# The last expert stage's first product for two batches at a time, as a 2x2x2 block product with seven products

## The chip, the core and the metric

The kernel runs on one core of one Trainium2 chip. The metric is device time in microseconds (us), the median of several runs of one kernel. Engines are called by the profile's names: PE (TensorE), DVE (VectorE), ACT (ScalarE), POOL (GpSimd) and SP (SyncE, which issues every DMA here).

## The reference

```python
x = attention(q, k, v)                   # 4 batches x 448 rows, 12 heads x 64 = 768 columns
h = x @ w_in;  g = h * cos(h)            # first expert stage, 768 -> 2048
y = g @ w_out                            # 2048 -> 768
a = y @ w1;  b = y @ w2                  # last expert stage, 768 -> 1024 each
out = ((a * b) @ w3) @ w_out2            # 1024 -> 1024 -> 768
```

All in float32. The host hands the weights over as 64-bit floats, which the kernel turns into float32 on the chip.

## The kernel before, in words

Data lie transposed: a tile has 128 columns of the activations as its partitions and the 448 rows of a batch along it. Every exact product is made of three matmuls on two-part numbers (`mm3`, lines 356 to 359): high weight by high data, high weight by low data, low weight by high data, 128 by 128 by 448 each. A high part is a copy to the `float32r` type (`copy`, line 331), a low part the difference (`lo`, line 349).

The program has three stretches: attention; the first expert stage (`moe1`, line 903), which works in units of two column blocks and one batch, first for batches 0 and 1, then for 2 and 3; and the last expert stage (`moe2`, line 1032). The product w3 by w_out2, called w34, is made during attention (`make_w34`) and kept in DRAM, so the last stage has two products: y by [w1|w2], then (a * b) by w34.

In the last stage `ab_unit` (line 1053) makes, for a batch b and a block fc of 128 columns, both a and b: six k-steps of three matmuls each, 18 matmuls to a PSUM bank and 36 to the unit. One bank is copied to `a32`, the other multiplied by it, and the result split into `ab` high and low. `o_unit` (line 1069) then adds ab by w34 into six PSUM banks, three matmuls to each, 18 to the unit; the banks are emptied to `ob` after the eighth block and written out. The order is batch 2, 3, 0, 1; unit fc of `ab` stands before `o_unit` of the unit ahead of it. The sums y of batches 2 and 3 are split where they arise (`split_y`, line 893, called in `y_part`); those of 0 and 1 come back from DRAM (`yA_d`) when their turn is near. The weights w1 and w2 are converted (`f64`, line 796: ACT or POOL, POOL or DVE, two DVE instructions, then the split) and stay in SBUF for all four batches, blocks 0 to 3 in the pool `lp`, early, the others in `q2`, whose space is free only when the first expert stage has ended. The same holds for w34.

PSUM has eight banks. Everything is issued in an order that a planner works out before (`Plan.schedule`, line 169): each operation has a due time, a list of engines that could do it with a cost on each, and the buffers it reads and writes; the planner walks through time and gives each engine the due operation that is ready. On the chip each engine goes through its own list strictly in that order, and semaphores hold an instruction until what it reads is there.

Of the kernel before, what the change touches and what calls it, by code (L numbers as in the profile page):

```python
# [10 lines left out]
F32 = mybir.dt.float32  # L11
F32R = mybir.dt.float32r
# [22 lines left out]
TWOPI = 6.283185  # L35

# [33 lines left out]
class Ring:  # L70
    def __init__(self, plan, pool, tag, shape, dtype, n):
        self.pool, self.tag, self.shape, self.dtype = pool, tag, list(shape), dtype
        self.tiles, self.queue = {}, []
        self.free = [(0.0, k) for k in range(n)]
        plan.rings.append(self)
        pool.rings.append(self)

    def tile(self, k):
        if k not in self.tiles:
            self.tiles[k] = self.pool.pool.tile(self.shape, self.dtype, name=f"{self.tag}{k}", bufs=1)  # L80
        return self.tiles[k]
# [226 lines left out]
def program(  # L308
# [47 lines left out]
    def mm3(out, wh, wl, xh, xl, first, last):  # L356
        PE.matmul(out, wh, xh, start=first, stop=False)  # L357
        PE.matmul(out, wh, xl, start=False, stop=False)  # L358
        PE.matmul(out, wl, xh, start=False, stop=last)  # L359
# [12 lines left out]
    for name, kw in dict(const={}, xring={}, dram=dict(space=DRAM), psum=dict(space=PSUM), attn={}, lp={},  # L372
                         wi=dict(side="right"), wp=dict(side="right"), yp=right, mp=right, cv=right,
                         qp=right, q2=right).items():
        pool(name, **kw)

    def ring(p, tag, shape, dtype=F32, n=2):
        return Ring(plan, pools[p], tag, shape, dtype, n)
# [48 lines left out]
    yA_d = Scratch("dram", [BH, KD, P, S], "yA_d")  # L427
# [27 lines left out]
    xh_r = ring("xring", "xh", [P, KD, S], F32R)  # L455
    xl_r = ring("xring", "xl", [P, KD, S], F32R)
# [339 lines left out]
    def f64(due, raw_r, x_r, src, n, hi, lw, spill=None):  # L796

        r = raw_r.ref()[:, :2 * n]
        x = x_r.ref()[:, :n]
# [24 lines left out]
        plan.op(due - 5, [("DVE", 0.07 + n / 960, low, True)], r=[r, x], w=[x])  # L824
        if spill is not None:
            dma(due - 4, spill, x, r=[x], w=[spill], kb=393, write=True)
# [12 lines left out]
    def hl(p, tag, shape, n):  # L839
        return [ring(p, tag + t, shape, F32R, n) for t in "hl"]  # L840
# [49 lines left out]

    yh, yl = {}, {}

    def split_y(b, m, due, src):
        if m == 0:
            yh[b], yl[b] = xh_r.new(), xl_r.new()
        th, tl = (z[b].at(m, lambda t: t[:, m, :]) for z in (yh, yl))
        copy(due, th, src, S, "ADP")
        lo(due, tl, src, th, S)
# [4 lines left out]
    def moe1(raw_r, x_r):  # L903
# [62 lines left out]
        def y_part(u, m, due):  # L966
# [18 lines left out]
            if u == of[b][-1] and b < BH:  # L985
                z = yA_d.at((b, m), lambda d: d[b, m])
                dma(due + 3, z, ya, r=[ya], w=[z], kb=230, write=True)
            if u == of[b][-1] and b >= BH:
                split_y(b, m, due + 2, ya)
# [40 lines left out]
    EARLY12, EARLY34 = 4, 2  # L1030

    def moe2():
        raw_r, x_r = ring("lp", "rawl", [P, 2 * DM], U32, 2), ring("lp", "xl_", [P, DM], F32, 2)
        a_r, ob_r = ring("qp", "a32", [P, S], F32, 2), ring("qp", "ob", [P, S], F32, 3)
        ab_r = hl("qp", "ab", [P, S], 2)
        V0, pu = unit_due(4 * NP) + G["pu"], G["pu"]
        order = [BH + r for r in range(BH)] + list(range(BH))
        w12t, w34t, ab, acc = {}, {}, {}, {}
        for k in range(2):
            for fc in range(NF2):  # L1040
                early = fc < EARLY12
                if early == (k == 0):
                    for a in range(2):
                        w12t[fc, a] = [ring("lp" if early else "q2", f"w12{t}{fc}{a}", [P, DM], F32R, 1).ref() for t in "hl"]
                        due = V0 - 90 + 20 * fc + 10 * a if early else V0 + (fc - 1) * pu / 2
                        f64(due, raw_r, x_r, w12[fc, a], DM, *w12t[fc, a])
                early = fc < EARLY34
# [115 lines left out]
```

## Time and profile before

| | us |
|---|---|
| median of three runs | 1142.82 (1141.08 to 1144.59) |
| span of the profiled execution, first to last instruction | 1139.2 |
| what lies around the span: the median less the span | 3.6 |
| PE busy in it | 1112.9 (98%) |
| DVE, ACT, POOL busy | 740.5, 454.2, 133.3 |

The page gives no time of its own for the profiled execution beside its span. A matmul row's duration holds its way through the array and overlaps the next one, so what a matmul costs is read from start to start. The span falls into attention with the making of w34 (to about 490 us), the first expert stage (to 781 us) and the last one (781 to 1131 us, then the last writes).

### The profile page before, as it was taken

The numbers are of one execution on the slowest core, as the hardware profiler recorded it, in microseconds if no ns is written. First come the engines' busy times: TensorE is split into PE (matmuls) and PEld (weight loads), VectorE is DVE, ScalarE is ACT, GpSimd is POOL, SyncE is SP. The second block draws the span as 40 slices with busy tenths as digits, with TensorE's granted clock in tenths as the row PEclk, the third lists the DMA queues.
The fourth block names the chain that finished last, engine by engine and source line by source line (L and its number), as shares of the span: only waits on it lengthen the run. The fifth ranks groups of instructions, "written<-read, shape, count | busy, mean of one in ns | idle before, by whom it ended". The sixth has DMA issues, their size and how long they took to land.

```text
span 1139.2 us, 13718 instructions
## 1 busy us (share of the span) xinstructions
PE 1112.9 (98%) x5184; PEld 966.5 (85%) x5184; DVE 740.5 (65%) x1111; ACT 454.2 (40%) x581; POOL 133.3 (12%) x130
## 2 busy tenths in 40 slices
PE   5999999999999999999999999999999999999997
PEld 3777777778888888889999999998999999999996
DVE  5888777899998897787899877768831311311111
ACT  4887767877566655722454211113211101101001
POOL 2312111123231110110121000001200000000000
PEclk9999999999999999999999999999999999999999
DMA  8885765878756554337745211101401101101001
GB/s 231 229 224 149 212 185 171 231 210 252 209 154 188 190 148 158 130 100 235 272 127 180 70 56 56 29 1 69 140 15 41 57 1 41 57 1 40 10 1 51
DMA packets 83165, 140.10 MB, mean 123 GB/s; under 512 B 35986, under 2 KB 63634, under 8 KB 83090
## 3 DMA queue, kind: packets, MB, share of 16 engines
q1 hardware_dynamic: 83090, 139.14, 40.7%
q8 instruction: 42, 0.69, 0.2%
q14 instruction: 33, 0.27, 0.1%
HBM read 109.45 MB, written 29.58 MB: 122 GB/s over the span
## 4 chain that ended last, share of the span: by engine, by line
PE 93%; DVE 2%; DMA 1%; ACT 1%; SPq 1%; issue 0%; POOL 0%; ACTq 0%; DVEq 0%
PE bank L357 13%; PE bank L358 13%; PE bank L359 13%; PE double L358 12%; PE double L359 12%; PE double L357 12%; PE bank L595 12%; PE double L574 3%; PE double L575 3%; DMA rawc<-in_w_out 1%; SPq L353 1%; DMA kr<-in_k 0%; DVE w L343 0%; ACT double L584 0%; ACT p L584 0%
## 5 line engine op out<-in xcount | busy, mean ns | idle before, releaser
L343 DVE TENSOR_TENSOR a<-double,a 128x448 f32<-128x448 f32 x32 | 20.0, 625 | 240.1 <-PE double L359 237.7
L595 PE MATMUL bank<-p,v 112*128 112x448 f32 x384 | 161.3, 543 | 0.5 <-issue 0.5
L359 PE MATMUL double<-xh,w12l 128*128 128x448 f32 x378 | 137.8, 365 | 0.0
L358 PE MATMUL double<-xl,w12h 128*128 128x448 f32 x378 | 137.8, 365 | 0.0
L357 PE MATMUL double<-xh,w12h 128*128 128x448 f32 x378 | 137.4, 363 | 0.0
L584 ACT ACTIVATE double<-double,ts 112x896 f32<-112x896 f32 x96 | 94.1, 981 | 79.1 <-PE double L575 78.9
L333 ACT COPY a<-double 128x448 f32<-128x448 f32 x31 | 16.5, 533 | 254.1 <-PE double L359 254.1
L357 PE MATMUL bank<-xh,wih 128*128 128x448 f32 x270 | 107.9, 399 | 0.0
L595 PEld LDWEIGHTS bank<-p,v 112*128 112x128 f32 x384 | 72.6, 190 | 41.2 <-issue 38.3
L357 PE MATMUL bank<-gh,woh 128*128 128x448 f32 x260 | 102.1, 393 | 0.3 <-ACT hs L333 0.3
L358 PE MATMUL bank<-xl,wih 128*128 128x448 f32 x270 | 98.3, 364 | 0.0
L359 PE MATMUL bank<-xh,wil 128*128 128x448 f32 x270 | 98.0, 363 | 0.0
L584 ACT ACTIVATE p<-double,pac 112x896 f32<-112x896 f32 x96 | 96.7, 1010 | 2.0
L358 PE MATMUL bank<-gl,woh 128*128 128x448 f32 x260 | 95.2, 366 | 0.0
L359 PE MATMUL bank<-gh,wol 128*128 128x448 f32 x260 | 94.8, 365 | 0.0
L574 PE MATMUL double<-qh,ks 128*112 128x448 f32 x192 | 73.7, 384 | 14.4 <-DVE ks L343 10.3
L343 DVE TENSOR_TENSOR y<-bank,y 128x448 f32<-128x448 f32 x111 | 68.6, 619 | 23.0 <-PE bank L359 22.2
L358 PEld LDWEIGHTS double<-xl,w12h 128*128 128x128 f32 x378 | 71.0, 188 | 5.8
L357 PEld LDWEIGHTS double<-xh,w12h 128*128 128x128 f32 x378 | 70.8, 187 | 5.6
L359 PEld LDWEIGHTS double<-xh,w12l 128*128 128x128 f32 x378 | 71.0, 188 | 5.0
L575 PE MATMUL double<-ql,ks 128*112 128x448 f32 x192 | 72.1, 375 | 0.0
L357 PEld LDWEIGHTS bank<-xh,wih 128*128 128x128 f32 x270 | 50.8, 188 | 9.0 <-issue 5.0
(153 smaller groups left out, 2359.2 us busy)
## 6 DMA issues: line engine op xcount, KB each, us to landing
rawc<-in_w_out SPq DMA_DIRECT2D x16, 768.0 KB, 5.6
rawl<-in_w SPq DMA_DIRECT2D x16, 768.0 KB, 4.4
qr<-in_q SPq DMA_DIRECT2D x48, 224.0 KB, 4.6
kr<-in_k SPq DMA_DIRECT2D x48, 224.0 KB, 4.9
rawc<-in_w_in SPq DMA_DIRECT2D x13, 768.0 KB, 5.0
raw<-in_w3T SPq DMA_DIRECT2D x16, 512.0 KB, 5.8
raw<-in_w_out SPq DMA_DIRECT2D x8, 768.0 KB, 7.2
wo_d<-wx SPq DMA_DIRECT2D x16, 384.0 KB, 4.4
```

Source lines behind the costliest of these rows:

```text
L333: "A": ("ACT", (0.051 if psum else 0.094) + n / 1200, lambda: ACT.copy(dst(), src())),
L343: "D": ("DVE", 0.068 + n / 960, lambda: DVE.tensor_tensor(dst(), a(), b(), op=op))
L353: plan.op(due, [("SP", 0.66, lambda: SP.dma_start(dst(), src()))], r=r, w=w, kb=kb)
L357: PE.matmul(out, wh, xh, start=first, stop=False)
L358: PE.matmul(out, wh, xl, start=False, stop=False)
L359: PE.matmul(out, wl, xh, start=False, stop=last)
L574: PE.matmul(o, w, qh(), start=True, stop=False)
L575: PE.matmul(o, w, ql(), start=False, stop=True)
L584: lambda f=f, x=x, o=o: ACT.activation(o(), s(), f, scale=x[:CP]))],
L595: PE.matmul(pv()[:, :S], w()[:, 2 * c + n].rearrange("p a d -> p (a d)"), p()[:, n, :], start=c == 0 and n == 0, stop=c == NT - 1 and n == 1)
```

## The change

y of two batches is taken as a matrix of 2 by 2 blocks: rows are the two batches, columns the halves of the 768 (three k-steps each). [w1|w2] of a block fc is the other: rows are the halves, columns w1 and w2. Their product, four banks of 18 matmuls times two batches before, is made from seven products of nine matmuls (`PRODUCTS`, in Winograd's form). The left operands `A11, A12, A22` are blocks of y, `S1` to `S4` sums of them, made once for each pair of batches (`lefts`); the right operands `B11, B21, B22` and `T1` to `T4` are made for each block fc, and again for the second pair (`rights`). Operands on both sides are split into high and low parts. The products are added up partly in PSUM, where a bank is read in between and then added to further (`ab_step`), and partly by DVE.

All four batches' y now go through DRAM (`y_d`). The converted w1 and w2 are written to DRAM for the first pair (`w12_d`) and read back for the second; w34 is read again for each of its 32 uses. Right operands lie in the ring `xring` (two slots), left ones in `lp` and `q2`. In the steps of a pair, `o_unit` of the pair's first batch goes between the products; its last block and all eight of the second batch follow after the pair's last step. Some tiles begin 64 bytes further on than their slot (`PAD // 2` of four bytes): the right operands, `A22` and `ab`. In the layout of the program before, start addresses modulo 128 bytes were 32 for y and for w1, w2 of blocks 0 to 3, and 96 for those of blocks 4 to 7, for `ab`, and for w34 of blocks 2 to 7 (32 for blocks 0 and 1). In the program now every moving operand of the last stage starts at 32 and every stationary one at 96.

```diff
-    def __init__(self, plan, pool, tag, shape, dtype, n):
...
+    def __init__(self, plan, pool, tag, shape, dtype, n, shift=0):
...
+        if not self.shift:
+            return self.flat(k)
+        t, n = self.flat(k), math.prod(self.shape[1:])
+        t = t[:, self.shift % PAD:self.shift % PAD + n]
...
+            shape = [self.shape[0], math.prod(self.shape[1:]) + PAD] if self.shift else self.shape
...
-    xh_r = ring("xring", "xh", [P, KD, S], F32R)
+    xh_r = ring("xring", "xh", [P, KD, S], F32R, 2, 0 if general else PAD)
...
-            if u == of[b][-1] and b < BH:
-                z = yA_d.at((b, m), lambda d: d[b, m])
+            if u == of[b][-1]:
+                z = y_d.at((b, m), lambda d: d[b, m])
                 dma(due + 3, z, ya, r=[ya], w=[z], kb=230, write=True)
-            if u == of[b][-1] and b >= BH:
...
+    KH, HALF = KD // 2, DM // 2
+    LEFT = ("A11", "A12", "S2", "S1", "S3", "S4", "A22")
+    RIGHT = ("B11", "B21", "T1", "T3", "T2", "T4", "B22")
+    PRODUCTS = (("A11", "B11"), ("A12", "B21"), ("S2", "T2"), ("S1", "T1"), ("S3", "T3"), ("S4", "B22"), ("A22", "T4"))
     def moe2():
...
+        raws = [ring("lp", "rawl", [P, 2 * DM], U32, 1), ring("q2", "rawq", [P, 2 * DM], U32, 1)]
+        sts = [ring("lp", "stl", [P, DM], F32, 4), ring("q2", "stq", [P, DM], F32, 2)]
+        left_r = {x: hl("q2" if x == "A22" else "lp", f"y{x}", [P, KH, S], 1, PAD // 2 * (x == "A22")) for x in LEFT}
+        w34_r, ab_r = hl("q2", "w34", [P, DM], 3), hl("q2", "ab", [P, S], 3, PAD // 2)
+        c_r, tmp_r, ob_r = (ring("q2", t, [P, S], F32, n) for t, n in (("c", 11), ("tmp", 6), ("ob", 5)))
+        V0, AB, OU = unit_due(4 * NP) + G["pu"], 63 * MM, 18 * MM
+        left, right, cs = {}, {}, {}
+        def lefts(p, due, step, raw_r, st_r, late=False):
...
+            for k in range(KH):
+                t = due + k * step
...
+                raw = raw_r.new()
+                a11, a21, a12 = (raw.at(n, lambda t, n=n: t[:, n * S:(n + 1) * S].bitcast(F32)) for n in range(3))
+                a22, s3 = st_r.ref()[:, :S], st_r.ref()[:, :S]
+                for x, n, m in ((a11, 0, k), (a21, 1, k), (a12, 0, k + KH), (a22, 1, k + KH)):
+                    load(x, n, m)
+                to("A11", a11, t)
+                to("A12", a12, t + 1)
+                tt(t + 2, s3, a11, a21, S, ALU.subtract, "PD")
+                tt(t + 2, a21, a21, a22, S, ALU.add, "PD")
+                tt(t + 3, a11, a21, a11, S, ALU.subtract, "PD")
+                tt(t + 4, a12, a12, a11, S, ALU.subtract, "PD")
+                to("S2", a11, t + 4)
+                to("S1", a21, t + 3)
+                to("S3", s3, t + 4)
+                to("S4", a12, t + 5)
...
+        def seg(z, i, n):
...
+            return z.ring.flat(z.slot)[:, PAD // 2 + i * HALF:PAD // 2 + (i + n) * HALF]
...
+        def rights(p, fc, due):
+            x = [sts[0].ref(), sts[0].ref()]
             for a in range(2):
+                z = w12_d.at((fc, a), lambda d, a=a: d[fc, a])
+                if p == 0:
+                    convert(due + 2 * a, raws[a if fc else 0], x[a], w12[fc, a], DM)
+                    dma(due - 4, z, x[a], r=[x[a]], w=[z], kb=393, write=True)
+                else:
+                    dma(due - 12, x[a], z, r=[z], w=[x[a]], kb=393)
+            t13, t24 = (sts[1 if fc or p else 0].ref() for _ in range(2))
...
+            (b11, b21), (b12, b22) = ((part(r, 0), part(r, 1)) for r in x)
+            (t1, t3), (t2, t4) = ((part(r, 0), part(r, 1)) for r in (t13, t24))
+            tt(due - 3, t1, b12, b11, HALF, ALU.subtract, "PD")
+            tt(due - 2, t3, b22, b12, HALF, ALU.subtract, "PD")
+            tt(due - 2, t2, b22, t1, HALF, ALU.subtract, "PD")
+            tt(due - 1, t4, b21, t2, HALF, ALU.subtract, "PD")
+            w = right[p, fc] = xh_r.new(), xl_r.new()
...
+            to(0, 2, x[0], due - 3)
+            to(6, 1, b22, due - 2)
+            to(4, 2, t24, due)
+            to(2, 2, t13, due - 1)
+        def product(p, fc, i, bank, first, due):
+            a, b = PRODUCTS[i]
+            j = RIGHT.index(b)
+            x, w = left[p, a], right[p, fc]
+            def f():
+                xt = [z.tile() for z in x]
+                wt = [seg(z, j, 1) for z in w]
+                for k in range(KH):
+                    c = slice(k * P, (k + 1) * P)
+                    mm3(bank()[:, :S], wt[0][:, c], wt[1][:, c], xt[0][:, k, :], xt[1][:, k, :],
+                        first and k == 0, k == KH - 1, on=not first)
+            plan.op(due, [("PE", 9 * MM, f)], r=[*(z.at(k) for z in x for k in range(KH)), *(z.at(2 * (j // 2)) for z in w)],
+                    w=[bank])
+        def ab_step(p, fc, due, between):
+            at = [due + i * (AB + OU) / 7 for i in range(8)]
...
+            p1 = hy_r.ref()
+            product(p, fc, 0, p1, True, at[0])
+            s1 = out(p1, at[1])
+            p2 = hy_r.ref()
+            product(p, fc, 1, p2, True, at[1])
+            c11 = c_r.ref()
+            tt(at[2], c11, p2[:, :S], s1, S, ALU.add, psum=True)
+            product(p, fc, 2, p1, False, at[2])
+            u2 = out(p1, at[3])
+            p3 = hy_r.ref()
+            product(p, fc, 3, p3, True, at[3])
+            s5 = out(p3, at[4])
+            product(p, fc, 4, p1, False, at[4])
+            tt(at[5], s5, p1[:, :S], s5, S, ALU.add, psum=True)
+            product(p, fc, 5, p3, False, at[5])
+            tt(at[6], u2, p3[:, :S], u2, S, ALU.add, psum=True)
+            tt(at[6] + 1, c11, c11, u2, S, ALU.mult, "DP")
+            product(p, fc, 6, p1, False, at[6])
+            c21 = c_r.ref()
+            tt(at[7], c21, p1[:, :S], s5, S, ALU.mult, psum=True)
+            cs[2 * p, fc], cs[2 * p + 1, fc] = c11, c21
+            for i, f in enumerate(between):
+                f(at[i + 1] + 0.1)
+        def o_unit(b, fc, due):
...
+            f32(due, sts[1], w34_d.at(fc, lambda d: d[fc]), DM, *w)
...
+        due = V0
+        lefts(0, unit_due(21), 14.0, raws[0], sts[0])
+        lefts(0, V0 + 2, 1.5, None, sts[1], late=True)
+        for p in range(2):
             for fc in range(NF2):
+                rights(p, fc, due - 4 if fc or p else due - 8)
+                ab_step(p, fc, due, o_unit(2 * p, fc - 1, due + 1) if fc else [])
+                due += AB + (OU if fc else 0)
+            if p == 0:
+                lefts(1, due, 7.0, raws[1], sts[0])
+                lefts(1, due + 15, 3.0, None, sts[0], late=True)
+            for b, fc in [(2 * p, NF2 - 1)] + [(2 * p + 1, fc) for fc in range(NF2)]:
+                for m, f in enumerate(o_unit(b, fc, due)):
+                    f(due + m * OU / KD)
+                due += OU
```

The order in which the engines get the work, at three places on DVE. A name's number tells tiles of one name apart.

First, DVE where the last stage begins. Before: `a` is the copy of the first bank, `xl` and `rawl` the weights under conversion.

```order
L334 CAST w34h_5532<-xl_3973 128x768
L343 TENSOR_TENSOR w34l_5536<-xl_3973,w34h_5532 128x768
L343 TENSOR_TENSOR w34l_5544<-xl_3942,w34h_5534 128x768
L817 SCALAR_TENSOR_TENSOR xl_3973<-rawl_3836,xl_3973 128x768
L817 SCALAR_TENSOR_TENSOR xl_3942<-rawl_3845,xl_3942 128x768
L343 TENSOR_TENSOR a_5560<-double_76,a_5560 128x448
L821 SCALAR_TENSOR_TENSOR xl_3973<-rawl_3836,xl_3973 128x768
```

Now: `tmp_5585` becomes S1T1 + S3T3 of the first block, `tmp_5583` the sum with S4B22, `yA22` is the operand of the first block's last product, `stl_4170` is w2 of the second block and `stq` its T blocks.

```order
L352 TENSOR_TENSOR tmp_5585<-bank_77,tmp_5585 128x448
L352 TENSOR_TENSOR yA22l_5614<-stq_5559,yA22h_5599 128x448
L352 TENSOR_TENSOR yA22l_5614<-stq_5563,yA22h_5599 128x448
L826 SCALAR_TENSOR_TENSOR stl_4170<-rawq_5546,stl_4170 128x768
L352 TENSOR_TENSOR tmp_5583<-double_75,tmp_5583 128x448
L830 SCALAR_TENSOR_TENSOR stl_4170<-rawq_5546,stl_4170 128x768
L352 TENSOR_TENSOR c_5561<-c_5561,tmp_5583 128x448
L352 TENSOR_TENSOR stq_5563<-stl_4170,stl_4016 128x384
L352 TENSOR_TENSOR stq_5563<-stl_4170 128x384
L343 CAST yA22h_5599<-stq_5559 128x448
L352 TENSOR_TENSOR xl_1091<-stl_4170,xh_1083 128x384
L352 TENSOR_TENSOR yA22l_5614<-stq_5559,yA22h_5599 128x448
```

The last third of A22 now stands behind a read of the bank that the fifth product fills, and behind part of the second block's conversion.

Second, DVE in the middle of the stage. Before, in the second half, between two units; `xl_452` is a split of the next batch's y:

```order
L343 TENSOR_TENSOR a_5560<-double_76,a_5560 128x448
L343 TENSOR_TENSOR xl_452<-ob_6119,xh_436 128x448
L343 TENSOR_TENSOR abl_5590<-a_5560,abh_5578 128x448
L343 TENSOR_TENSOR a_5618<-double_76,a_5618 128x448
L334 CAST abh_5627<-a_5618 128x448
L343 TENSOR_TENSOR abl_5633<-a_5618,abh_5627 128x448
```

Now, in one step of the first pair, from the fourth block's second product on (`c` collects a, `xl` are low halves of right operands):

```order
L352 TENSOR_TENSOR c_5927<-bank_80,tmp_5587 128x448
L830 SCALAR_TENSOR_TENSOR stl_4010<-rawq_5546,stl_4010 128x768
L352 TENSOR_TENSOR stq_5559<-stl_4010,stl_4002 128x384
L352 TENSOR_TENSOR stq_5559<-stl_4010 128x384
L352 TENSOR_TENSOR stq_5563<-stl_4010,stq_5559 128x384
L352 TENSOR_TENSOR xl_453<-stl_4010,xh_437 128x384
L352 TENSOR_TENSOR stq_5563<-stl_4002,stq_5563 128x384
L352 TENSOR_TENSOR xl_453<-stq_5559,xh_437 128x768
L826 SCALAR_TENSOR_TENSOR stl_4016<-rawl_3844,stl_4016 128x768
L352 TENSOR_TENSOR xl_453<-stq_5563,xh_437 128x768
L352 TENSOR_TENSOR tmp_5684<-double_76,tmp_5684 128x448
```

Reads of PSUM banks (`c`, `tmp`) now stand between conversions and splits of the next block's operands, 21 instructions to a step of 81 matmuls.

Third, DVE between the two halves of the stage. Before, at the change of batch, `xh` and `xl` are the next batch's y:

```order
L343 TENSOR_TENSOR abl_5633<-a_5618,abh_5627 128x448
L334 CAST xh_436<-ob_6106 128x448
L343 TENSOR_TENSOR xl_452<-ob_6106,xh_436 128x448
L343 TENSOR_TENSOR xl_452<-ob_6112,xh_436 128x448
L343 TENSOR_TENSOR xl_452<-ob_6119,xh_436 128x448
```

Now, while PE works through the second batch of the first pair, the last third of the next pair's left operands:

```order
L343 CAST w34h_5784<-stq_5559 128x768
L352 TENSOR_TENSOR rawq_5546<-rawq_5546 128x448
L352 TENSOR_TENSOR yS1l_4073<-rawq_5546,yS1h_4071 128x448
L352 TENSOR_TENSOR yA12l_3982<-rawq_5546,yA12h_3970 128x448
L352 TENSOR_TENSOR yS3l_4024<-stl_4010,yS3h_4014 128x448
L352 TENSOR_TENSOR rawq_5546<-rawq_5546 128x448
L343 CAST yA22h_5599<-stl_4016 128x448
L352 TENSOR_TENSOR yS2l_4085<-rawq_5546,yS2h_4075 128x448
L352 TENSOR_TENSOR yA22l_5614<-stl_4016,yA22h_5599 128x448
L352 TENSOR_TENSOR yS4l_4096<-rawq_5546,yS4h_4087 128x448
L352 TENSOR_TENSOR yA22l_5614<-stl_4170,yA22h_5599 128x448
L352 TENSOR_TENSOR w34l_5797<-stq_5559,w34h_5784 128x768
```

The low part of a w34 block that PE is about to use now stands behind splits for the next pair.

## Rows read from the trace of the kernel before

**Rows 1.** Chain of work that ended last: share of the span by engine.
```profile
PE 93%; DVE 2%; DMA 1%; ACT 1%; SPq 1%; issue 0%; POOL 0%; ACTq 0%; DVEq 0%
```

**Rows 2.** Windows: PE, PEld, DVE, ACT, POOL busy (instructions), granted clock, DMA, GB/s.
```profile
500.00:600.00 100.00, 100.00 (x495) 92.52 (x494) 88.30 (x130) 36.86 (x53) 15.67 (x14) 1.00 0.61 204
...
800.00:850.00 50.00, 50.00 (x249) 46.28 (x248) 30.53 (x38) 8.25 (x13) 6.73 (x6) 1.00 0.27 87
...
900.00:950.00 50.00, 50.00 (x251) 46.62 (x250) 7.17 (x13) 2.66 (x5) 0.00 (x0) 1.00 0.00 1
```

**Rows 3.** What PE waited for: us in total, times, longest.
```profile
PE double L574 <- DVE ks L343: 10.3, 1, 10.3
...
PE double L358 <- DVE gl L343: 2.6, 1, 2.6
```

**Rows 4.** PE in order of time, last stage: start, duration, what.
```profile
781.39 0.36 PE L357 MATMUL bank<-xh,w12h 128*128 128x448 f32 x1
...
788.82 0.37 PE L357 MATMUL double<-xh,w12h 128*128 128x448 f32 x1
...
796.26 0.37 PE L357 MATMUL bank<-abh,w34h 128*128 128x448 f32 x1
...
799.90 0.37 PE L357 MATMUL double<-xh,w12h 128*128 128x448 f32 x1
...
822.06 0.37 PE L357 MATMUL double<-xh,w12h 128*128 128x448 f32 x1
...
829.27 0.36 PE L357 MATMUL bank<-abh,w34h 128*128 128x448 f32 x1
...
1130.86 0.37 PE L359 MATMUL double<-abh,w34l 128*128 128x448 f32 x1
```

**Rows 5.** DVE in order of time, last stage.
```profile
797.81 0.63 DVE L343 TENSOR_TENSOR abl<-a,abh 128x448 fp32r<-128x448 f32 x1
798.35 0.95 DVE L817 SCALAR_TENSOR_TENSOR xl<-rawl,xl 128x768 uint32<-128x768 uint32 x1
799.34 0.96 DVE L821 SCALAR_TENSOR_TENSOR xl<-rawl,xl 128x768 uint32<-128x768 uint32 x1
800.33 0.56 DVE L334 CAST w12h<-xl 128x768 fp32r<-128x768 f32 x1
800.80 0.56 DVE L334 CAST w34h<-xl 128x768 fp32r<-128x768 f32 x1
801.27 0.95 DVE L343 TENSOR_TENSOR w12l<-xl,w12h 128x768 fp32r<-128x768 f32 x1
802.14 0.95 DVE L343 TENSOR_TENSOR w34l<-xl,w34h 128x768 fp32r<-128x768 f32 x1
...
804.86 1.56 DVE L821 SCALAR_TENSOR_TENSOR xl<-rawl,xl 128x768 uint32<-128x768 uint32 x1
```

**Rows 6.** DVE by form: count, busy us, mean ns, idle before.
```profile
L343 DVE TENSOR_TENSOR a<-double,a 128x448 f32<-128x448 f32 x32 | 20.0, 625 | 240.1 <-PE double L359 237.7 <-ACT w12h L333 2.4
...
L343 DVE TENSOR_TENSOR sum<-bank,sum 128x384 f32<-128x384 f32 x16 | 8.8, 550 | 3.3 <-PE bank L359 3.2
```

**Rows 7.** DMA issues: count, KB each, median us to landing.
```profile
ob<-yA_d SPq DMA_DIRECT2D x12, 224.0 KB, 2.8
```

**Rows 8.** POOL in order of time, last stage.
```profile
804.72 0.88 POOL L805 TENSOR_SCALAR rawl<-rawl 128x768 f32<-128x768 f32 x1 [0.89 <-DMA rawl<-in_w]
```

**Rows 9.** DVE in order of time, end of the first expert stage.
```profile
771.86 1.15 DVE L343 TENSOR_TENSOR xl<-y,xh 128x448 fp32r<-128x448 f32 x2
772.93 1.08 DVE L343 TENSOR_TENSOR gl<-w,gh 128x896 fp32r<-128x896 f32 x1
```

**Rows 10.** ACT in order of time, end of the span; in brackets the idle time before.
```profile
1132.98 0.53 ACT L333 COPY ob<-double 128x448 f32<-128x448 f32 x1 [0.26 <-DMA outT<-ob]
```

**Rows 11.** PE in order of time, start of the span.
```profile
10.80 0.57 PE L575 MATMUL double<-ql,ks 128*112 128x448 f32 x1
11.17 0.57 PE L574 MATMUL double<-qh,ks 128*112 128x448 f32 x1
```

More of the change, by code (lines that the diff above doesn't have):

```diff
@@ L35 @@
 TWOPI = 6.283185
+PAD = 32
 class Ref:
@@ L354, in dma, with mm3 @@
                 kb=kb)
[L356 to L359, printed above, removed]
+    def mm3(out, wh, wl, xh, xl, first, last, on=False):
+        PE.matmul(out, wh, xh, start=first, stop=False, skip_group_check=on)
+        PE.matmul(out, wh, xl, start=False, stop=False, skip_group_check=on)
+        PE.matmul(out, wl, xh, start=False, stop=last, skip_group_check=on)
     MM = S / 2400 + 0.017
@@ new lines, in ab_step, with out @@
+        def ab_step(p, fc, due, between):
+            at = [due + i * (AB + OU) / 7 for i in range(8)]
+            def out(bank, when):
+                x = tmp_r.ref()
+                copy(when, x, bank[:, :S], S, "AD", psum=True)
+                return x
+            p1 = hy_r.ref()
[21 more added lines that the diff above has]
+                f(at[i + 1] + 0.1)
@@ new lines, in moe2, with one, go, f @@
+        acc = {}
+        def o_unit(b, fc, due):
+            w, ab = pair(w34_r), pair(ab_r)
+            f32(due, sts[1], w34_d.at(fc, lambda d: d[fc]), DM, *w)
+            halves(due - 1.5, ab, cs[b, fc], S)
+            def one(m):
+                def go(at):
+                    if fc == 0:
+                        acc[m] = hy_r.ref()
+                    o = acc[m]
+                    def f():
+                        mm3(o()[:, :S], w[0]()[:, m * P:(m + 1) * P], w[1]()[:, m * P:(m + 1) * P], ab[0](), ab[1](),
+                            fc == 0, fc == NF2 - 1)
+                    plan.op(at, [("PE", 3 * MM, f)], r=[*w, *ab], w=[o])
+                    if fc == NF2 - 1:
+                        ob = ob_r.ref()
+                        copy(at + 0.6, ob, o[:, :S], S, "AD" if m % 2 else "DA", psum=True)
+                        dma(at + 1.5, Ref(out_i, (b, m)).view(lambda _: outT[b, m]), ob,
+                            r=[ob], w=[Ref(out_i, (b, m))], kb=230, write=True)
+                return go
+            return [one(m) for m in range(KD)]
@@ L1088, in moe2 @@
         out_i = Item(None)
         out_i.tile = lambda: None
-        prev, due = None, V0
-        for n, b in enumerate(order):
+        due = V0
+        lefts(0, unit_due(21), 14.0, raws[0], sts[0])
+        lefts(0, V0 + 2, 1.5, None, sts[1], late=True)
+        for p in range(2):
             for fc in range(NF2):
-                ab_unit(b, fc, due)
-                due += 6.8
-                if prev is not None:
-                    o_unit(*prev, due)
-                    due += 3.4
-                prev = (n, b, fc)
-                if n >= 1 and n + 1 < B and fc < KD:
-                    nb = order[n + 1]
-                    yr = ob_r.ref()
-                    src = yA_d.at((nb, fc), lambda d, nb=nb, fc=fc: d[nb, fc])
-                    dma(due - 4, yr, src, r=[src], w=[yr], kb=230)
-                    split_y(nb, fc, due + 4, yr)
@@ L1118, in program @@
             f()
-    for n in ("q2", "qp", "lp", "psum", "dram", "xring", "const"):
+    for n in ("q2", "lp", "psum", "dram", "xring", "const"):
         pools[n].close()
```

110 lines of the change are left out of this document (39 added, 71 removed).

## The prediction, made before the changed kernel ran

> **What bounds the kernel now.** I read first the chain of work that ended last: 93% of it is PE [rows 1]. Then PE's waits: 10.3 us at the very start, 2.6 us at the end of the first expert stage, none in the last one [rows 3]. The windows show a granted clock of 1.00, and DVE busy for 30.53 and 7.17 of 50 us in the last stage; in attention it has 88.30 of 100 while PE has 100.00 [rows 2]. PE in order of time gives the stage itself: from the first matmul at 781.39 to the last start at 1130.86 there are 1727 distances in 349.5 us, 202.4 ns each [rows 4]. The last stage is a row of matmuls without a hole; it costs their number times their distance.
>
> **What goes.** For a and b a unit has 36 matmuls, 32 units 1152; `o_unit` adds 18 each, 576: together 1728. Seven products of nine matmuls make 63 where two units took 72, so 1008 replace 1152 and the stage has 1584. The 144 removed are worth 144 x 0.2024 = 29.1 us, all on PE and so on the path.
>
> **What a matmul costs.** The distance is not one number. From 788.82 to 796.26 36 matmuls take 206.7 ns each; both operands start there at the same remainder modulo 128 bytes. From 822.06 to 829.27, weights at 96 and y at 32, 36 take 200.3 ns; the 18 of `o_unit` from 796.26 to 799.90, remainders also apart, take 202.2 [rows 4]. Now all are apart. I take 0.2003 for the products, 1008 x 0.2003 = 201.9, and 0.201, between 0.2003 and 0.2022, for the other 576, 115.8: 317.7 us. Against 349.7 (1728 x 0.2024) that is 32.0 us, of which 2.9 come from the distance. This second term may be nothing (1584 x 0.2024 = 320.6): that the remainders cause the difference is read from two stretches, and DMA or DVE traffic could have caused it too.
>
> The Trainium skill speaks against it: "SBUF — State Buffer", section "Who interferes with whom", gives PE one read port for the moving operand and an independent one for weight loads, and says that PE never waits on anyone. By that rule start addresses would not matter and the sum would be 2.9 us longer. The trace's 206.7 and 200.3 do not fit it unless something else parts them.
>
> **What is added.** Prices on DVE, start to start where one does not wait for the one ahead: 0.54 us for 448 columns, 0.87 for 768, 0.47 for a cast of 768; by size some 0.47 for 384. A conversion instruction (`STT` here, for SCALAR_TENSOR_TENSOR) takes 0.95, 0.99 where the next needs its result [rows 5]. A bank read of 448 takes 0.62 by duration, of 384 0.55 [rows 6]; start to start I take 0.54.
>
> *Start of the stage.* Call PE's first matmul there 0. The first block's fifth product (S3T3) ends 63 matmuls in, since two products of the second block stand ahead of it: 12.6 us. DVE's first row in the first place shown in the order waits for it. Behind it until the last third of A22 stand: two A22 lows (2 x 0.54), STT 0.95, bank read 0.54, STT 0.99, c 0.62, two of 384 (0.94), a cast 0.40 (by size from 0.47), 384 0.47, and the low itself 0.62; with the first read some 7.2 us, so it is ready at 19.8. The last product begins at 72 matmuls, 14.4 us, and needs that third after six more, at 15.6: PE waits 4.2 us. A22's third piece is read from DRAM once a slot is free; by the reads of 2.8 us [rows 7] it comes in time. DVE goes on through T2 and T4 of the second block and their low parts, another 5.3 us, to 25.1; the second block's T2 product wants them at 22.6: 2.5 us. Together 6.7, between 3 (DVE reaches the place with less behind it) and 10 (a load late by its own 2.8).
>
> *Steps of the first pair.* A step has 81 matmuls, 16.2 us. DVE has 21 rows: five STT (4.65), four of 768 (3.48), five of 384 (2.35), four bank reads (2.16), two of 448 (1.12), a cast (0.47): 14.2 us if nothing waits, 16.2 by durations. DVE at nearly 90% beside a full PE exists in attention [rows 2], so I take the seven steps as covered but for 2 us, with 0 and 12 as ends (the second is worked out under the rivals).
>
> *Between the pairs.* PE works through nine `o_unit` (32 us), which is DVE's time for the second pair's left operands. DVE's own list from the last product of the first pair on has 42 rows up to the low part of w34 for the sixth of these blocks, 23.7 us by the prices above; that puts it at 150.1 us after the stage's begin, where PE wants it at 148.9: 1.2 us late. By durations, some 0.09 longer each, it would be 5.0 late. I take 3; the ends are 0 and, with DVE 3 us behind when it gets there, 8.
>
> *Second pair.* No conversions; DVE has 11 to 12 of 16.2 us. What is left are the banks: three matmul groups wait in turn for a read of the bank they add to. I take 1, from 0 to 4.
>
> *At the ends.* At the end of the first expert stage five `xl` of y2's kind (two halves in 1.15 us [rows 9]) no longer stand ahead of `gl`, for which PE waits 2.6 [rows 3]: minus 1, from minus 2.6 to nothing. The last copies wait 0.26 us for a free `ob` [rows 10] with three slots; now there are five, and the five writes start nearer to the last matmul: minus 1, from minus 1 to nothing. DVE's work in front of the stage is as much as before.
>
> *Sum.* 1139.2 (span) - 32.0 + 6.7 + 2 + 3 + 1 - 1 - 1 = 1117.9. The median lies 3.6 us above the span of the profiled execution, so 1121.5: I predict 1122. With all waits at their lower ends (3, 0, 0, 0) and minus 2.6 and minus 1 it is 1106.6 + 3.6 = 1110.2. With the upper ends (10, 12, 8, 4) and no gain from the distance it is 1139.2 - 29.1 + 34 + 3.6 = 1147.7.
>
> One thing could add: the granted clock. After the 10.3 us without matmuls at the start they went 0.37 us apart [rows 11], near the level of 1.2 GHz; after the gap of 2.6 us no lower clock was granted (1.00 in the windows, [rows 2, 3]). The gaps of 4.2 and 2.5 us lie between, nearer the second; I add nothing.
>
> **Rivals.** (1) *DVE bounds the first pair.* At 804.72 POOL runs a conversion of 0.88 us, and DVE's STT at 804.86 takes 1.56 in place of 0.96 [rows 5, 8]. In attention POOL and DVE run together too and PE is not held [rows 2], but POOL has only 14 instructions in 100 us there. A step now has about 3.4 on POOL, most of 768 columns; if each costs DVE 1 us, 14.5 + 3.4 = 17.9 against 16.2, 1.7 a step, seven steps 12 in place of 2: 1132. "SBUF — State Buffer" of the Trainium skill, in the same section, states such a lock (a DVE instruction with two SBUF inputs against a GpSimd one that reads SBUF, the second waiting for the whole of the first); the trace's 1.56 agrees.
>
> (2) *The waits are covered.* Buffers and PE's list let work flow past the holes; lower ends everywhere: 1111. For it speaks DVE's 7.17 of 50 us before; against it, that at the start the order itself fixes 7 us behind one bank.
>
> (3) *No gain from the distance:* 2.9 us more, 1125.
>
> (4) *Slower: the banks.* Six of the eight banks hold sums of ab·w34 through a batch, so only two serve the seven products. A bank that PE adds to again must be read within the next 9 to 12 matmuls, 1.8 to 2.4 us; the read takes 0.62 [rows 6], with the handovers some 1.0, but DVE may be inside an STT of 0.95 or, with POOL in it, 1.56 [rows 5]. Of the 112 products the 96 that are not at a batch's beginning would wait 0.4 us each (1.0 + 1.56 - 2.1): 38 us, 1122 + 38 - 2 = 1158. It makes the kernel slower from some 0.27 us a product. Against it: the upper end holds only if a long instruction stands in front of nearly every read, and part of the reads are ACT's.
>
> **How the numbers follow.** Forecast 0.50, with 1115 to 1128 as its own range; rival 1 0.18; 2 0.12; 3 0.12; 4 0.08. The range is 1111 to 1140: it takes in the lower end and all but rival 4 and the far part of rival 1. 0.3% is 3.4 us, what a measurement of this kernel can tell from no change. Slower than 1146.2 is little but rival 4, 0.08. Within 1139.4 and 1146.2 lie the tails of rivals 1 and 4, 0.05. Faster 0.87.
>
> **What would show it.** The list of PE's groups should have 1008 and 576 matmuls, some 200 ns apart in a stretch without waits; 206 there would refute the distance. PE's waits should be for `yA22` and a low part `xl` in the first 25 us of the stage, for `w34l` between the pairs, none of over a microsecond in the second pair. DVE should be near 90% in the first pair's windows; at 98%, with PE waiting for `xl` in every step, rival 1 holds; many short waits of PE for `tmp` or `c` are rival 4. The forecast falls if the stage's matmuls end later than 332 us after its first (317.7 + 12.7 + 1.6), or if the stretch before it has changed by over 5 us.

## The result and the profile after

| | before | after |
|---|---|---|
| median | 1142.74 us (4 runs, 1141.08 to 1144.59) | 1125.30 us (4 runs, 1121.52 to 1126.89) |
| ratio | | 0.9838, 95% interval 0.9824 to 0.9852 |
| span of the profiled execution | 1139.2 us | 1125.1 us |
| last stage, first to last start on PE | 349.47 us, 1728 matmuls | 332.42 us, 1584 matmuls |

The changed kernel is 1.6% faster. Forecast was 1122, range 1111 to 1140. The stage was forecast with 317.7 + 12.7 = 330.4 us. The prediction had named 332 as the length at which it falls, and the stage's 332.42 passes that by 0.4: a term in the stage's sum was wrong, and the runs below show which.

PE's waits after the change, in us: total, times, longest (for [rows 3]):

```profile
PE bank L366 <- DVE yA22h L343: 2.8, 1, 2.8
PE bank L368 <- DVE w34l L352: 1.7, 1, 1.7
...
PE double L368 <- DVE w34l L352: 1.1, 1, 1.1
...
PE double L366 <- ACT tmp L342: 0.6, 1, 0.6
...
PE double L367 <- DVE abl L352: 0.4, 1, 0.4
PE double L367 <- DVE gl L352: 0.4, 1, 0.4
PE bank L367 <- DVE yA22l L352: 0.3, 1, 0.3
```

`yA22` is the wait at the start of the stage; of the two for `w34l` one is in the third step and one between the pairs. The `gl` wait ahead of the stage has shrunk from 2.6 to 0.4 us. There is no crowd of waits for `tmp` or `c`.

PE in order of time shows these places (for [rows 4]): start, duration, what, and in brackets the idle time before and what ended it.

```profile
784.17 0.36 PE L366 MATMUL bank<-yA11h,xh 128*128 128x448 f32 x1
...
798.73 0.36 PE L366 MATMUL bank<-yA22h,xh 128*128 128x448 f32 x1
...
799.75 0.37 PE L368 MATMUL bank<-yA22h,xl 128*128 128x448 f32 x1
802.90 0.74 PE L366 MATMUL bank<-yA22h,xh 128*128 128x448 f32 x1 [2.78 <-DVE yA22h L343]
803.90 0.74 PE L367 MATMUL bank<-yA22l,xh 128*128 128x448 f32 x1 [0.26 <-DVE yA22l L352]
...
804.81 0.58 PE L366 MATMUL bank<-yS1h,xh 128*128 128x448 f32 x1
...
807.80 0.58 PE L368 MATMUL bank<-yS1h,xl 128*128 128x448 f32 x1
...
809.59 0.37 PE L366 MATMUL double<-yS2h,xh 128*128 128x448 f32 x1
...
811.60 0.47 PE L366 MATMUL double<-yS3h,xh 128*128 128x448 f32 x1 [0.62 <-ACT tmp L342]
...
827.94 0.47 PE L368 MATMUL double<-abh,w34l 128*128 128x448 f32 x1 [1.08 <-DVE w34l L352]
...
921.62 0.47 PE L367 MATMUL double<-abl,w34h 128*128 128x448 f32 x1 [0.44 <-DVE abl L352]
...
945.44 0.47 PE L368 MATMUL bank<-abh,w34l 128*128 128x448 f32 x1 [1.73 <-DVE w34l L352]
...
1116.59 0.37 PE L368 MATMUL bank<-abh,w34l 128*128 128x448 f32 x1
```

Read the distances. 784.17 to 798.73 is 72 matmuls, 202.2 ns each, not 200.3. From 804.81 to 807.80 eight matmuls take 374 ns each: that is the lower clock level of 1.2 GHz, as in [rows 11], and it lasts until 809.59. The granted clock in the windows agrees, and the windows also show the first pair's steps (columns as in [rows 2]):

```profile
800.00:825.00 25.00, 21.34 (x88) 18.35 (x88) 24.18 (x38) 11.16 (x16) 5.55 (x4) 0.86 0.54 179
...
850.00:875.00 25.00, 25.00 (x125) 23.12 (x124) 22.82 (x33) 9.70 (x15) 5.06 (x5) 1.00 0.53 181
```

The granted clock is 0.86 in the first one. In the second, DVE is busy for 22.82 of 25 us, and PE still does not wait.

### The profile page after: what moved, and what is told of

It reads as the page before. It is cut to its first block, busy times and chain, and to the rows that moved or that the text cites. A ratio compares the mean times of both kernels' runs of the same rounds, so it can differ in the third digit from the quotient of the medians.

```text
span 1125.1 us, 13995 instructions
## 1 busy us (share of the span) xinstructions
PE 1091.6 (97%) x5040; PEld 941.1 (84%) x5040; DVE 889.7 (79%) x1353; ACT 498.6 (44%) x656; POOL 153.3 (14%) x145
## 5 line engine op out<-in xcount | busy, mean ns | idle before, releaser
L366 PE MATMUL bank<-w2h,w3h 128*128 128x384 f32 x128 | 57.6, 450 | 1.7 <-ACT sum L342 1.7
L367 PEld LDWEIGHTS bank<-xl,wih 128*128 128x128 f32 x270 | 50.9, 188 | 9.3 <-issue 5.2
L819 POOL TENSOR_SCALAR wx<-rawc 128x768 f32<-128x768 f32 x29 | 34.7, 1195 | 168.0 <-DVE wil L352 65.8
L342 ACT COPY hs<-bank 128x448 f32<-128x448 f32 x39 | 20.8, 533 | 80.9 <-PE bank L368 80.9
L366 PEld LDWEIGHTS bank<-gh,woh 128*128 128x128 f32 x260 | 48.9, 188 | 8.7 <-issue 2.8
L367 PEld LDWEIGHTS bank<-gl,woh 128*128 128x128 f32 x260 | 49.0, 188 | 7.2 <-issue 3.5
L368 PEld LDWEIGHTS bank<-xh,wil 128*128 128x128 f32 x270 | 50.7, 188 | 3.9
L964 ACT ACTIVATE w<-w 128x896 f32<-128x896 f32 x32 | 30.5, 954 | 50.5 <-DVE w L352 50.4
```

The source lines that it names most:

```text
L342: "A": ("ACT", (0.051 if psum else 0.094) + n / 1200, lambda: ACT.copy(dst(), src())),
L366: PE.matmul(out, wh, xh, start=first, stop=False, skip_group_check=on)
L367: PE.matmul(out, wh, xl, start=False, stop=False, skip_group_check=on)
L368: PE.matmul(out, wl, xh, start=False, stop=last, skip_group_check=on)
L819: lambda: POOL.tensor_scalar(x(), h_().bitcast(F32), 0.0, 1.0, op0=ALU.mult, op1=ALU.mult)),
L964: plan.op(due + 5, [("ACT", 0.094 + 2 * S / 1200, lambda: ACT.activation(w2(), w2(), AF.Sin, scale=TWOPI))], r=[w2], w=[w2], table="sin")
```

## Experiments

All ratios are to the kernel before. An experiment on the changed kernel is to be compared with that kernel's 0.9838. A distance is the time from one matmul's start to the next one's.

**e1, equal remainders.** The right operands start 64 bytes lower, which makes the remainder 32 on both sides of all 1008 product matmuls.

```diff
-            return z.ring.flat(z.slot)[:, PAD // 2 + i * HALF:PAD // 2 + (i + n) * HALF]
+            return z.ring.flat(z.slot)[:, i * HALF:(i + n) * HALF]
```

> The changed kernel with its right operands (the stationary ones of the seven products) 64 bytes further down, so that all 1008 product matmuls have both operands at remainder 32 modulo 128; the order on every engine is the same. Theory of the prediction (equal remainders cost some 6 ns a matmul): products 206 to 207 ns apart, 1008 x 6.4 ns = 6.5 us longer, 1131 to 1132 us. Rival (the remainders mean nothing, the two stretches of before differed by something else): products stay at 202 to 203 ns, within 0.3% of 1125.

Measured: 1126.85 us, ratio 0.9861 (0.9846 to 0.9876). The first 72 matmuls of the stage:

```profile
780.35 0.36 PE L366 MATMUL bank<-yA11h,xh 128*128 128x448 f32 x1
...
794.91 0.36 PE L366 MATMUL bank<-yA22h,xh 128*128 128x448 f32 x1
```

That is 14.56 us for 72, exactly as with the shift. Over the stage, leaving out distances over 0.25 us, products stand 203.0 ns apart here and 202.8 in the changed kernel. The equal remainders cost 0.2 ns, not the 6 of the theory; the rival holds.

**e2, one product twice.**

```diff
             product(p, fc, 0, p1, True, at[0])
+            product(p, fc, 0, p1, True, at[0])
```

> The changed kernel with the first of the seven products made twice in each of the 16 steps (the second time overwrites the first): as many matmuls as before the change, 1728, with all else of the change kept. If PE alone bounds the steps: 144 x 0.2024 = 29 us longer less what waits it covers, 1148 to 1154 us, slower than before the change. Rival (DVE bounds the first pair, or waits take the place of products): under 15 us longer, below 1140.

Measured: 1150.96 us, ratio 1.0067 (1.0051 to 1.0082), 25.7 us more than the changed kernel. The stage is 359.90 us long (782.56 to 1142.46), 27.5 more. So the 144 matmuls are worth what PE takes for them (144 x 0.2023 = 29.1 us), less 1.6 us of waits that the longer step covers. With as many matmuls as before, the new form is 7.7 us slower than the kernel before (1143.30 beside this run): that is its overhead.

**e3, A22 first.**

```diff
-                    a22 = st_r.ref()[:, :S]
+                    a22 = c_r.ref() if p == 0 else st_r.ref()[:, :S]
...
-        lefts(0, V0 + 2, 1.5, None, sts[1], late=True)
+        lefts(0, V0 - 2, 0.4, None, sts[1], late=True)
```

> Only the loads and splits of A22 of the first pair go ahead, into their own buffers, so that DVE has them done before it reads the bank of the fifth product. If that place in DVE's list was the whole cause of the stage's first wait (2.95 us and 3.4 us of lower clock after it): 6 us shorter, 1119. Rival (DVE is behind as a whole there, because the second block is converted only after the stage has begun): the wait passes on to the low parts xl of that block's T1 and T2, 4 to 6 us long, the granted clock falls after it as well, and the time stays within 3 us of 1125.

Measured: 1129.10 us, ratio 0.9882 (0.9866 to 0.9898), slower than the changed kernel. PE there:

```profile
803.88 0.74 PE L366 MATMUL bank<-yS1h,xh 128*128 128x448 f32 x1 [5.01 <-ACT xh L342]
...
806.17 0.74 PE L368 MATMUL bank<-yS1h,xl 128*128 128x448 f32 x1 [1.17 <-DVE xl L352]
```

A22 is no longer waited for; the operand T1 of the second block is, for longer, and the clock falls again (0.74 us rows). The rival's mechanism holds: moving one instruction group forward only passes the wait on. Its time, within 3 us of 1125, was passed by 1 us.

**e4, the second block's conversion before the stage**, in addition to e3's edit.

```diff
-                    convert(due + 2 * a, raws[a if fc else 0], x[a], w12[fc, a], DM)
+                    convert(due + 2 * a, raws[a if fc > 1 else 0], x[a], w12[fc, a], DM)
...
-            t13, t24 = (sts[1 if fc or p else 0].ref() for _ in range(2))
+            t13, t24 = (sts[1 if fc > 1 or p else 0].ref() for _ in range(2))
...
-                rights(p, fc, due - 4 if fc or p else due - 8)
+                rights(p, fc, due - (8 if p == fc == 0 else 12 if p == 0 and fc == 1 else 4))
```

> As the last, and in addition the second block's w1 and w2 are converted before the stage begins, in the buffers that are free then. Both theories of the first wait expect no wait at the stage's start; if the clock stays at 1.00 then, 2.95 + 0.9 us of waits and 3.4 us of lower clock go, 7 us: 1118. If the conversions only move the wait to the end of the first expert stage (gl, 0.8 us now): 1121 to 1123.

Measured: 1115.59 us, ratio 0.9756 (0.9740 to 0.9771), 9.7 us less than the changed kernel. In the first 25 us of the stage only one short wait is left:

```profile
803.56 0.48 PE L366 MATMUL double<-yS3h,xh 128*128 128x448 f32 x1 [0.62 <-ACT tmp L342]
```

and PE's waits as a whole have no `yA22` any more:

```profile
PE bank L368 <- DVE w34l L352: 1.7, 1, 1.7
PE bank L366 <- ACT hs L342: 0.9, 1, 0.9
PE bank L367 <- DVE xl L352: 0.7, 1, 0.7
```

The stage takes 324.46 us (782.72 to 1107.18), 8.0 less: 6.6 at its start, where the wait for A22 and the lower clock behind it are gone, and 1.35 in the third step, where the wait for `w34l` is gone too. The other 1.7 us of the medians' difference lie outside the stage and have no shown cause. Nothing new is seen at the end of the first expert stage. This version beats both kernels.

**e5, the kernel before again**, unchanged.

> The kernel before once more, for its profile. Open is why matmuls of the first expert stage, which the change leaves alone, stood 202.3 to 202.6 ns (h) and 204.5 to 204.8 ns (y) apart in five profiles with the change and 201.3 and 203.7 in the one of before. If this is an execution's own speed, this profile may show 202.4 and 204.6 too, and the last stage 1728 matmuls about 203.3 ns apart, 351 us; if the change itself slows these matmuls, it shows 201.3 and 203.7 again and 349.5 us.

Measured: 1145.91 us, span 1143.8. The stage lasts 349.47 us again (785.56 to 1135.03), to the last digit of the first profile. The matmuls of the first expert stage's product h stand 201.2 ns apart and those of y 204.3, counting distances up to 0.25 us between two of one kind; counted so they are 201.4 and 203.9 in the first profile of before and 202.4 and 204.7 in the changed kernel's. So the last stage of before repeats, neither of the two answers fits y, and h bears out the second. The surprise is PE behind the `gl` wait:

```profile
776.74 0.47 PE L358 MATMUL double<-gl,woh 128*128 128x448 f32 x1 [2.58 <-DVE gl L343]
777.05 0.36 PE L359 MATMUL double<-gh,wol 128*128 128x448 f32 x1
...
778.36 0.58 PE L359 MATMUL double<-gh,wol 128*128 128x448 f32 x1
...
781.66 0.36 PE L359 MATMUL bank<-gh,wol 128*128 128x448 f32 x1
```

The same place in the first profile of before:

```profile
774.07 0.47 PE L358 MATMUL double<-gl,woh 128*128 128x448 f32 x1 [2.58 <-DVE gl L343]
774.38 0.36 PE L359 MATMUL double<-gh,wol 128*128 128x448 f32 x1
774.58 0.37 PE L357 MATMUL double<-gh,woh 128*128 128x448 f32 x1
```

The gap is 2.58 us in both. In one execution the clock stays up, in the other the lower level (0.58 rows) follows for 3.3 us. The profile of e9, below, has this gap too, and the lower level behind it (374 ns a matmul from 776.14 to 779.13).

**e6, e4 without moving A22** (the three edits shown under e4 alone).

> The second block's w1 and w2 converted before the stage as in e4, A22 left where the change has it. If DVE's queue as a whole made the first wait (as e3 says), A22 is in time in its old place as well: within 2 us of e4, 1114 to 1118. If A22's place costs something of its own beside it: 2.95 us and perhaps 3.4 us of lower clock come back, 1119 to 1122.

Measured: 1118.42 us, ratio 0.9781 (0.9763 to 0.9798). The stage takes 325.00 us, 0.5 more than in e4, and has no wait for `yA22`. In the profile A22's place costs almost nothing once DVE is not behind. The medians lie 2.8 us apart, with intervals that overlap; what makes the rest was not found.

**e7, w34 earlier**, in addition to e4.

```diff
-            f32(due, sts[1], w34_d.at(fc, lambda d: d[fc]), DM, *w)
+            f32(due - 3, sts[1], w34_d.at(fc, lambda d: d[fc]), DM, *w)
```

> e4, and in addition the loads and splits of w34 are due 3 us earlier, so that DVE has them ahead of the next pair's left operands. Waits between the pairs of 0.6, 1.9 and 0.2 us and the one of 0.3 us at the end should go: 3 us, 1112 to 1113. Rival: the splits of the second pair become late in their turn, or operands of a block in the first pair; no gain, 1115 to 1117.

Measured: 1116.28 us, ratio 0.9752 (0.9738 to 0.9766), the same as e4. The wait for `w34l` is gone, but at that place PE now waits 1.2 us for `abl`, another low part in the same list of DVE. The stage is 0.7 us shorter (323.76), where 3 us were expected, so the rival is nearer.

**e8, more work on DVE**, in addition to e4, in six steps.

```diff
             lo(due + 0.5, z[1], src, z[0], n)
+            if twice:
+                lo(due + 0.5, z[1], src, z[0], n, "D")
```

> e4, and in six of the first pair's steps the four subtractions that make low parts of the right operands are done once more on DVE: 3 x 0.87 + 0.47 = 3.1 us of further work in a step of 16.4 us. If DVE has the 2 us of room a step that its 89% busy (of 20 us, 17.9) show: 6 x 1.1 = 5 to 7 us longer than e4, less what is held in advance, 1117 to 1123. If DVE and POOL hold each other up so that DVE is already the bound (rival 1 of the prediction): 6 x 3.1 = 18 us, 1134.

Measured: 1124.26 us, ratio 0.9825 (0.9809 to 0.9841), 8.7 us more than e4 and 1 above the expected 1117 to 1123; the stage takes 331.00 us, 6.5 more. DVE is full and PE now has holes:

```profile
850.00:875.00 25.00, 24.29 (x119) 22.00 (x119) 24.95 (x34) 8.00 (x13) 7.06 (x6) 1.00 0.53 181
```

Of 18.5 us of work put on DVE, 6.5 came through to the stage's length: 2 us a step were covered. So DVE did not bound the steps, but it would be the next to do so, some 2 us away.

**e9, the kernel before with its first blocks' weights 64 bytes further on.**

```diff
-                        w12t[fc, a] = [ring("lp" if early else "q2", f"w12{t}{fc}{a}", [P, DM], F32R, 1).ref() for t in "hl"]
+                        w12t[fc, a] = [ring("lp" if early else "q2", f"w12{t}{fc}{a}", [P, DM], F32R, 1, PAD // 2 if early else 0).ref() for t in "hl"]
```

> The kernel before with w1 and w2 of blocks 0 to 3 placed 64 bytes further on, so that all 1152 matmuls of y by [w1|w2] have the moving operand at remainder 32 and the stationary one at 96; the order is the same. If the remainders matter in this kernel (its first blocks stood 206.7 ns apart at 32 and 32, blocks 4 and 5 200.3 at 32 and 96): the first blocks go to 200 to 201 ns, the mean of 1152 from 202.3 to 200.5, 2 us shorter. If, as in e1, they mean nothing: 206 to 207 ns at the same place, 202.3 on the mean, within 0.3% of the kernel before.

Measured: 1142.48 us, ratio 0.9985 (0.9974 to 0.9995). PE at the stage's start:

```profile
783.90 0.36 PE L368 MATMUL bank<-xh,w12h 128*128 128x448 f32 x1
...
791.18 0.36 PE L368 MATMUL double<-xh,w12h 128*128 128x448 f32 x1
```

36 matmuls take 7.28 us, 202.2 ns each; in [rows 4] the same 36, from 781.39 to 788.82, took 206.4. Unit by unit, blocks 0 to 3 stand at 202.1 to 202.5 in every batch. Before, seven units of this sort stood at 206.4 to 206.7 (the four of the first batch and the first of each later one) and nine at 202.6 to 202.7, all with equal remainders. Blocks 4 to 7 stand at 200.2 to 200.3 in both. The stage is 348.32 us, 1.15 less. So these start addresses cost 4 ns in some units and next to nothing in others. What makes 200.3 in place of 202.4 is something else, which goes with blocks 4 to 7, whose weights lie in the other pool. Neither expected answer was right as a whole. The edit also makes each of these slots 128 bytes longer, so all tiles but the first move by more than 64 bytes; no run parts the remainder from the place.

## Why the prediction was right, and which step of it failed

*The number of matmuls.* 29.1 us, right: e2 brings the 144 back for 27.5 us of stage.

*What a matmul costs: failed.* The prediction took "0.2003 for the products" from a stretch of blocks 4 and 5, on the reading that unequal remainders made it. e1 makes the remainders equal and changes nothing; e9 makes them unequal in the kernel before and reaches 202.1 to 202.5, not 200.3. The products stand 202.8 ns apart; the mean of all 1555 undisturbed distances, up to 0.25 us, is 202.3. In place of 2.9 us the term gave 0.2. That is rival 3, no gain from the distance. The rule that stood beside it, from "SBUF — State Buffer" of the Trainium skill, section "Who interferes with whom" (PE never waits on anyone), agrees with e1 (203.0 against 202.8 ns). It does not cover e9, where another start address took 4 ns from a matmul in seven units; there the measurement decides.

*Start of the stage: right in place and nearly in size; the clock took the place of the second wait.* DVE's list in order of time:

```profile
797.11 0.63 DVE L352 TENSOR_TENSOR tmp<-bank,tmp 128x448 f32<-128x448 f32 x1 [3.94 <-PE bank L368]
...
802.46 0.38 DVE L343 CAST yA22h<-stq 128x448 fp32r<-128x448 f32 x1
802.76 0.55 DVE L352 TENSOR_TENSOR xl<-stl,xh 128x384 fp32r<-128x384 f32 x1
803.23 0.62 DVE L352 TENSOR_TENSOR yA22l<-stq,yA22h 128x448 fp32r<-128x448 f32 x1
```

The read of the fifth product's bank begins 12.9 us into the stage and the last A22 low ends at 803.85, 19.7 us in; forecast were 12.6 and 19.8. PE's two holes there, 3.15 and 1.00 from start to start, take 3.7 us beside their two matmuls (4.2 forecast). The second forecast wait, 2.5 us for T2, did not come: PE had been slowed until DVE was ready. That is where the step "I add nothing" for the clock failed: from 803.90 to 809.59 14 distances take 5.69 us instead of 2.83, 2.9 us lost. The step leaned on one execution, in which 2.58 us without matmuls left the clock up (the windows of [rows 2] do not reach that place; PE's rows under e5 do). e5 shows the same gap followed by the lower level: 9 distances in 3.30 us, 1.5 us lost.

In the sum the lower clock cost next to nothing here, as far as two executions can tell. e1 has the same order and the same hole, but the lower level lasts 3.4 us there, and PE then waits for the low part of T2:

```profile
799.08 0.47 PE L366 MATMUL bank<-yA22h,xh 128*128 128x448 f32 x1 [2.79 <-DVE yA22h L343]
...
800.60 0.57 PE L366 MATMUL bank<-yS1h,xh 128*128 128x448 f32 x1
...
803.96 0.39 PE L366 MATMUL double<-yS2h,xh 128*128 128x448 f32 x1
...
805.23 0.47 PE L368 MATMUL double<-yS2h,xl 128*128 128x448 f32 x1 [0.67 <-DVE xl L352]
```

With 0.9 us at 811.60, a handover of a bank by way of ACT, the stretch from 799.75 to 811.91 lost 12.16 - 23 x 0.2023 = 7.5 us in the changed kernel; the same 23 distances of e1, from 795.92 to 807.85, lost 7.3. So a lower clock for 3.4 us more changed the sum by 0.2 us: it filled time in which PE would have waited for DVE. Without the handover, which no term of the prediction had, 6.6 us are left; 6.7 were forecast, all of it as waits. That e4 gives 6.6 us back here shows the cause: DVE's list, which holds the second block's conversion, and not the place of A22 in it (e3, e6).

*Steps of the first pair: right in size, without its cause.* 1.35 us were lost (827.94), 2 forecast. DVE has 22.82 of 25 us, 91%, beside a full PE; e8 shows that 2 us a step of room were left. The one wait is for a `w34l` that took 2.62 us in place of 0.95, while POOL had an instruction of its own:

```profile
825.27 2.62 DVE L352 TENSOR_TENSOR w34l<-stq,w34h 128x768 fp32r<-128x768 f32 x1
```
```profile
824.96 2.11 POOL L354 TENSOR_TENSOR xl<-stl,xh 128x768 fp32r<-128x768 f32 x1 [1.77 <-ACT xh L342]
```

DVE's instruction ends at 827.89, 0.8 us after POOL's. This is the meeting of rival 1. Other DVE instructions met POOL as well (a conversion at 822.38 takes 1.63 in place of 0.95), but PE waits for one only, and not in every step.

*Between the pairs: right.* 0.6 us at 921.62 and 1.9 at 945.44, together with the next distances 2.7 against 3. The larger one is `w34l`, as forecast. What stands behind it in DVE's list is the next to be late (e7).

*Second pair:* 0.6 us, 1 forecast; no chain of waits for banks.

*The ends: one better, one wrong.* `gl` gave 2.2 us, not 1. The tail gave nothing, where 1 us was forecast: from the last start to the end of the span 8.34 us before and 8.51 after. What fills it was not tested.

*What no step had.* The stage of the profiled execution begins at 784.17, 2.8 us later than in the first profile of before, though `gl` is earlier. 2.8 us are there by 240 us, 2.3 of them in two places at which PE waits near the start of the first expert stage. e5, the kernel before, has the same two, and the first profile of before has neither:

```profile
225.06 0.47 PE L366 MATMUL bank<-xh,wih 128*128 128x448 f32 x1 [0.80 <-DVE xh L343]
...
235.65 0.47 PE L366 MATMUL bank<-gh,woh 128*128 128x448 f32 x1 [0.96 <-ACT hs L342]
```
```profile
224.74 0.47 PE L357 MATMUL bank<-xh,wih 128*128 128x448 f32 x1 [1.20 <-DVE xh L334]
...
235.33 0.47 PE L357 MATMUL bank<-gh,woh 128*128 128x448 f32 x1 [1.01 <-ACT hs L333]
```

So these waits differ between executions of one kernel. Another 2.1 us gather evenly between 235 and 690 us: h, counted as under e5, stands 202.4 to 202.5 ns apart in the profiles of the changed kernel, of e1 to e4 and of e6 to e8, against 201.4, 201.2 and 201.4 in the two profiles of before and in e9. These matmuls, their order and their remainders are unchanged; some of their moving operands begin 128 to 384 bytes further on, because the ring they lie in is padded. The 2.1 us go with the changed kernel, and their cause is open.

*Rivals.* 1 (DVE bound): not so. (Its price is also too high by its own rows: the prediction's DVE time in a step is 14.2 us, and the rival goes on with 14.5.) POOL and DVE do meet, and both pay: DVE in the `w34l` above, POOL here:

```profile
807.97 3.11 POOL L819 TENSOR_SCALAR stl<-rawq 128x768 f32<-128x768 f32 x1 [10.93 <-ACT rawq L813]
```

3.11 us for what takes POOL 0.88 at other places, while DVE's conversions at 807.18 and 808.91 take 0.95 and a split at 808.04, between them, 0.95. By the same section of the Trainium skill whoever issues second waits for the whole of the other's instruction. The trace agrees for the `w34l`; POOL's 2.2 us of delay are more than one of DVE's instructions. 2 (covered): no, 12.1 us are lost in the stage over 0.202 a matmul. 3 (no gain from the distance): its term was right; that the time came out at its 1125 needs the other deviations below to cancel but for 1 us. 4 (banks): a single wait of 0.62 us for `tmp` in the whole stage.

*The sum.* The stage is 2 us over its forecast: 2.7 for the distance, 0.8 at the start (for the most part the handover by way of ACT), minus 1.3 for the steps, the stretch between the pairs and the second pair. Ahead of it 2.1 us came that no step had; `gl` and the tail cancel. So the direction and the size rest on the count of matmuls, which held, and 1125.3 in place of 1121.5 is the failed distance and the open 2.1 us for the most part.

That the median is only 3.8 us over is partly luck. The span of the profiled execution, 1125.1, is 7.2 over its forecast of 1117.9: the 2.8 us by 240 us are in it as well. What brings it back is the term of 3.6 us for what lies around the span, and no run shows that much around it. In every execution whose time and span are both on record the two differ by 1.7 to 2.1 us. The rest of the 3.6 is that the profiled execution of before was faster than the median, without the two waits above, while that of the changed kernel is the slowest of its four (1126.89 us). Before, the step from the profiled span to the median was 3.6 us; after, it is 0.2.

## What to carry to other kernels

Take a term from a difference between two stretches only after asking what else differs between them; here the block, its pool and its place in the batch did as well as the remainder. Changing the start address by itself was worth 4 ns in some units and nothing in the products. A late operand is read from the whole list of the engine that makes it: putting one instruction ahead in a full list moves the wait to the next one, and the gain comes from taking work out of that stretch. A hole of some 3 us on PE can have the lower clock behind it; whether that adds to the time depends on whether PE would have waited for the late engine anyway. And a sum that starts from a profiled span must ask whether that execution was a typical one.

## What the runs showed of the hardware

- A gap of 2.58 us on PE was followed by the lower level of 1.2 GHz in e5 and e9 and not in the first profile of before, at the same place. After 3.15 us from start to start the level was lower until 809.59 in the changed kernel (374 ns a matmul in place of 202); after 3.16 us in e1, whose order is the same, it was lower from 800.60 to 804.0 only. Holes of 0.99 us in e4 (803.56) and 2.09 us at 945.44 in the changed kernel, from start to start, were not followed by it; two of 1.02 and 1.63 us close together in e2 (805.50 and 807.43) were, from 808.56 to 815.46.
- Another start address of the weights: 206.4 to 206.7 against 202.1 to 202.5 ns in seven units of the kernel before (e9), 202.8 against 203.0 in the products after (e1).
- POOL and DVE held each other up: 2.62 us for a split that takes DVE 0.95, and 3.11 us for a conversion that takes POOL 0.88.
- One and the same row of 147 matmuls of ab by w34 between the pairs (142 distances up to 0.25 us) stood 200.2 ns apart in the changed kernel's profile, 200.1 in e4 and 203.3 in e1, the order on every engine being that of the changed kernel in e1. Whether the execution makes this or e1's other start addresses is open.
